# Two engines share each copy of the first transform's results, one parity each

## The chip, the cores and the metric

The kernel runs as one program on one core of a Trainium2 chip. The metric is the device time of that core in microseconds (us), the median of several runs. A core has five engines that each work through a queue of their own in order: TensorE (PE in the profile; its weight loads are listed as PEld), VectorE (DVE), ScalarE (ACT), GpSimd (POOL) and SyncE (SP), which here only starts transfers. They meet through semaphores. Matrix products land in PSUM; everything else on the core lies in SBUF; transfers between SBUF and the device's memory run on 16 DMA engines.

## The reference

The input x has 8 batches of 3136 positions by 256 channels. The attention part is the real part of a two-dimensional Fourier transform of each batch. Behind it each batch sends the 128 positions with the highest gate score through a small feed-forward network:

```
X = np.fft.fft(x, axis=1)
X = np.fft.fft(X, axis=2)
x = X.real
scores = np.einsum('bsd,d->bs', x, w_gate)
for b in range(B):
    top_idx = np.argpartition(-scores[b], capacity)[:capacity]   # capacity = 128
    xe = x[b, top_idx]
    ye = np.maximum(xe @ w1, 0.0) @ w2
    out[b, top_idx] = xe + sigmoid(scores[b, top_idx])[:, None] * ye
```

## The kernel before

The sequence of 3136 positions is split as 64 by 49, so the transform has three matrix products per batch.

**First transform** (`stage1`, lines 354 to 387). A batch of x arrives as four transfers of 1 MB (`load_to`, line 206). Mirrored rows are added in place (`fold_to`, line 345: VectorE for batch 0, GpSimd for the others). There are eight chunks per batch; each is multiplied with `w1d` into one PSUM bank `p1_{batch}_{chunk}` of 4 times 100 columns (line 372; the last chunk has 5 times 100). The 100 columns are two parities h by two halves t by 25 frequencies k. Line 373 copies a bank into the tile `uv`, in which each k has a row of 64, so neighbouring elements of the copy land 256 bytes apart. The last chunk has a second, small copy (line 375, 100 elements). The tile `zz` (line 381) holds a small side product of the same batch.

**Second and third transform** (`stage23`, line 390). Line 405 multiplies `uv` with `cuv`, six or four products to a bank. ScalarE rounds the bank to `s2h` (line 410), VectorE subtracts to get the rest `s2l` (line 411), and three products (lines 244 to 246) give the result, which VectorE or ScalarE copies to the output tile `o` (line 423). GpSimd adds a correction and the score (lines 428 to 434), SyncE stores.

**Search for the best 128** (`topk`, line 468, one per pair of batches, called A, B, C, D here). It narrows a threshold in six rounds. In the first three groups a round goes round the engines: ScalarE counts with a pass of 800 elements (`junk`, line 531, and `cth`, 532), PE sums over the partitions (`pc`, line 541), VectorE decides (`ji`, line 543) and sets the next threshold (`thr`, line 547). The next round's ScalarE pass waits for that threshold.

**Feed-forward network** (`ffn`, line 639), for pairs of batches.

A string written out by hand (`ORDER`, line 37) says in which order the pieces of these streams are written down, and so in which order each engine meets them. Nothing is reordered later: an instruction that waits holds up all that stand behind it on its engine. Seven PSUM banks are taken in turn (line 189). The first matrix product of the second transform of a batch needs the whole tile `uv`, with the copies of all eight chunks and line 375.

Of the kernel before, what the change touches and what calls it, by code (L numbers as in the profile page):

```python
# [177 lines left out]
def kernel(ctx: ExitStack, tc: tile.TileContext, x, w1, w2, wgr, tb, outs, groups, pairs):  # L178
    nc = tc.nc
# [12 lines left out]
    def bank(name, pool=psb):  # L192
        return pool.tile([128, 512], F32, tag="bank", name=name)
# [5 lines left out]
    def load_to(q):  # L199
        while len(tiles) <= min(q, 4 * NB - 1):  # L200
            b, i = divmod(len(tiles), 4)
            t = xp.tile([128, 2, 8 * 128], F32, tag="x", name=f"x_{b}_{i}")
            tiles[b, i] = t
            src = x[b, i].rearrange("p (c w) -> p c w", c=2)
            for c0, c1 in ((0, 1), (1, 2)) if b == 0 else ((0, 2),):
                nc.sync.dma_start(t[:, c0:c1], src[:, c0:c1])
# [128 lines left out]
    def fold_to(q):  # L335
        while len(folded) <= min(q, 8 * NB - 1):
            b, i = divmod(len(folded), 8)
            if i == 0:
                zs[b] = sp.tile([98, 33], F32, tag="z", name=f"z_{b}", bufs=2)
            z = zs[b]  # L340
            a0, a1 = CHUNKS[i]
            n = a1 - a0
            t = tiles[b, i // 2][0:98, i % 2]
            eng = nc.vector if b == 0 else nc.gpsimd
            eng.tensor_tensor(t[:, 0 : n * 128], t[:, 0 : n * 128], t[:, n * 128 : 2 * n * 128], op=ALU.add)  # L345
            if i % 2:
                d = tiles[b, i // 2][0:98].rearrange("p c (s d) -> p c s d", d=128)
                nc.gpsimd.tensor_copy(z[:, a0 - 4 : a0 + 4].rearrange("p (c s) -> p c s", c=2), d[:, :, 0:4, 0])  # L348
            if i == 7:
                nc.gpsimd.tensor_copy(z[:, 0:33:32], d[:, 1, 6:8, 0])  # L350
            folded.append(t)


    def stage1(b):

        uv = uvp.tile([128, 2, 25, 64], F32, tag="uv", name=f"uv_{b}")
        uvs[b] = uv
        uvt = uv.rearrange("p h k (t n) -> p h t n k", t=2)
        for i in range(8):
            if i % 2 == 0:  # L360
                load_to(4 * b + i // 2 + AHEAD)
            fold_to(8 * b + i + FOLDS)
            t = folded[8 * b + i]
            a0, a1 = CHUNKS[i]
            n = a1 - a0
            ps = bank(f"p1_{b}_{i}")[:, 0:500].rearrange("p (n c) -> p n c", n=5)
            src = ps.rearrange("p n (h t k) -> p h t n k", h=2, t=2)

            for q in range(5 if i == 7 else n):
                o = (q + 3 if i == 7 and q > 2 else q) * 128  # L370
                for r in (0, 64):
                    nc.tensor.matmul(ps[r : r + 64, q], t[:, o + r : o + r + 64], w1d, start=True, stop=True)  # L372
            nc.scalar.copy(uvt[:, :, :, a0:a1], src[:, :, :, 0:n])  # L373
            if i == 7:
                nc.scalar.copy(uvt[:, :, :, 0], src[:, :, 0, 3:5])  # L375
            yield True

        pz = bank(f"pz_{b}")[:, 0:500].rearrange("p (n c) -> p n c", n=5)
        nc.tensor.matmul(pz[0:33, 0, 0:50], zs[b], w1d[:, 50:100], start=True, stop=True)
        zz = sp.tile([33, 50], F32, tag="zz", name=f"zz_{b}", bufs=2)  # L380
        nc.scalar.copy(zz, pz[0:33, 0, 0:50])
        yield True
        nc.tensor.matmul(pz[:, 1, 0:25], zcs[:, 0:128], zz[:, 25:50], start=True, stop=False)
        nc.tensor.matmul(pz[:, 1, 0:25], zcs[:, 128:256], zz[:, 0:25], start=False, stop=True)
        nc.scalar.copy(dlt[b % 2][0], pz[:, 1, 0:25])
        nc.scalar.activation(dlt[b % 2][1], pz[:, 1, 0:25], AF.Copy, scale=wodd)
        yield True
# [305 lines left out]


    streams = {"s": (c for b in range(NB) for c in stage1(b)), "m": (c for b in range(NB) for c in stage23(b)), "w": late_setup()}
    for g, bs in enumerate(groups):
        streams["ABCD"[g]] = topk(g)
# [57 lines left out]
```

## Time and profile before

| what | value |
|---|---|
| median of 3 runs | 249.34 us (249.08 to 251.72) |
| the profiled execution's own time | 248.94 us |
| its span, first to last instruction | 247.2 us |
| PE, DVE, ACT, POOL busy share of the span | 90%, 55%, 56%, 65% |
| mean granted TensorE clock, share of full | 0.939 |
| memory traffic | 67.40 MB |

The busy shares are means over the whole span. The eight first transforms run up to about 165 us; what follows is the rest of the last batch, the search D and the feed-forward networks. Matrix products are pipelined and their ends are modelled, so a PE that reads as busy need not be at its peak.

### The profile page before, as it was taken

The page shows a single profiled execution, that of the slowest core. Times are in us where ns is not written, and L with a number is a line of the kernel's source. Part 1 is how long each engine was busy: PE and PEld are TensorE (multiplying, and loading weights), DVE is VectorE, ACT ScalarE, POOL GpSimd, SP SyncE. Part 2 cuts the span into 40 slices and gives each one's busy share as a digit, 9 for nine tenths or more (in the row PEclk, how much of TensorE's full clock was granted, in tenths as well). Part 3 has the DMA queues.
Part 4 walks back from the last instruction along what each step waited for, and adds up shares of the span by engine and source line. Part 5 has one row for each costly group of instructions (what it writes and reads, how often), then busy time and mean ns, then how long its engine had stood idle before and what let it go on. Part 6 is the DMA issues. An engine that isn't in the chain of part 4 may idle for free.

```text
span 247.2 us, 6813 instructions
## 1 busy us (share of the span) xinstructions
PE 221.3 (90%) x2672; PEld 199.8 (81%) x2672; DVE 134.8 (55%) x422; ACT 137.4 (56%) x309; POOL 160.2 (65%) x233
## 2 busy tenths in 40 slices
PE   8769999999999989997998995989999899998950
PEld 5559899989989879897987783979889798997940
DVE  1533332443553444657585558374689998943410
ACT  2544767757755887882677865877851140312300
POOL 0026799898797767965867999447958436446141
PEclk9976999999999999997999999558999999999995
DMA  6999959999999999999999899543068402011000
GB/s 226 386 407 399 400 217 361 384 414 404 406 417 319 424 405 417 414 400 399 416 420 402 301 335 382 241 160 127 0 265 248 165 22 54 26 32 43 24 22 23
DMA packets 14908, 67.40 MB, mean 273 GB/s; under 512 B 3131, under 2 KB 4892, under 8 KB 11292
## 3 DMA queue, kind: packets, MB, share of 16 engines
q1 hardware_dynamic: 13740, 64.80, 67.0%
q0 software_dynamic: 1024, 2.13, 3.4%
q8 instruction: 21, 0.34, 0.6%
q10 hardware_dynamic: 112, 0.04, 0.1%
q14 instruction: 11, 0.09, 0.1%
HBM read 39.17 MB, written 27.79 MB: 271 GB/s over the span
## 4 chain that ended last, share of the span: by engine, by line
PE 40%; DMA 25%; DVE 16%; POOL 5%; ACT 5%; issue 5%; POOLq 1%; SPq 1%; ACTq 0%
DMA spill<-sc 11%; PE p L405 10%; PE p L372 10%; DMA scr<-spill 5%; DMA xe<-out,chosen 4%; PE p L244 4%; DMA once<-in_once 3%; DMA x<-in_x 3%; PE p L246 3%; DVE junk L534 3%; PE p L245 3%; DVE o L423 2%; DVE hl L674 2%; DVE s2l L411 2%; ACT uv L373 2%
## 5 line engine op out<-in xcount | busy, mean ns | idle before, releaser
L345 POOL TENSOR_TENSOR x<-x 98x512 f32<-98x512 f32 (+1 forms) x56 | 68.9, 1245 | 8.8 <-DMA x<-in_x 7.9
L372 PE MATMUL p<-w1d,x 98*64 98x100 f32 x1056 | 58.6, 266 | 4.6 <-DVE x L345 3.4
L411 DVE TENSOR_TENSOR s2l<-p,s2h 128x390 fp32r<-128x390 f32 (+1 forms) x72 | 36.2, 530 | 46.9 <-ACT s2h L410 46.3
L373 ACT COPY uv<-p 128x400 f32<-128x400 f32 x64 | 50.5, 859 | 18.8 <-PE p L372 18.8
L372 PEld LDWEIGHTS p<-w1d,x 98*64 98x64 f32 x1056 | 52.0, 147 | 8.6 <-DVE x L345 3.7
L405 PE MATMUL p<-cuv,uv 128*64 128x130 f32 x800 | 54.7, 288 | 2.3 <-ACT uv L375 1.3
L405 PEld LDWEIGHTS p<-cuv,uv 128*64 128x64 f32 x800 | 47.3, 144 | 5.2 <-ACT uv L375 1.8
L428 POOL TENSOR_TENSOR o<-o,dl 128x384 f32<-128x384 f32 (+1 forms) x32 | 27.6, 862 | 19.3 <-DVE o L423 12.7
L410 ACT CAST s2h<-p 128x390 fp32r<-128x390 f32 (+1 forms) x72 | 31.7, 469 | 11.8 <-PE p L405 11.4
L688 POOL DMA_INDIRECT out<-xe,chosen x16 | 15.7, 980 | 22.4 <-DMA out<-xe,chosen 16.6
L423 DVE COPY o<-p 128x390 f32<-128x390 f32 (+1 forms) x48 | 23.6, 512 | 12.1 <-PE p L246 9.0
L244 PE MATMUL p<-s2h,m3h 128*128 128x390 f32 (+1 forms) x72 | 27.5, 382 | 0.2 <-ACT s2h L410 0.2
L246 PE MATMUL p<-s2l,m3h 128*128 128x390 f32 (+1 forms) x72 | 24.4, 339 | 0.0
L245 PE MATMUL p<-s2h,m3l 128*128 128x390 f32 (+1 forms) x72 | 24.1, 335 | 0.0
L531 ACT ACTIVATE junk<-scr,thr 128x800 bf16<-128x800 f32 x18 | 17.3, 962 | 10.0 <-DVE thr L547 8.9
L673 ACT ACTIVATE hh<-ph 128x256 fp32r<-128x256 f32 x32 | 12.2, 383 | 17.3 <-PE ph L246 16.6
L650 POOL DMA_INDIRECT xe<-out,chosen x16 | 15.8, 986 | 9.4 <-DVE hl L674 4.8
L244 PE MATMUL ph<-xh,w1h 128*128 128x256 f32 x64 | 19.0, 297 | 0.0
L246 PE MATMUL ph<-xl,w1h 128*128 128x256 f32 x64 | 18.3, 285 | 0.0
L245 PE MATMUL ph<-xh,w1l 128*128 128x256 f32 x64 | 18.1, 282 | 0.0
L348 POOL COPY z<-x 98x8 f32<-98x8 f32 x32 | 6.2, 195 | 16.5 <-DVE x L345 14.7
L244 PEld LDWEIGHTS p<-s2h,m3h 128*128 128x128 f32 x72 | 13.9, 193 | 3.4 <-ACT s2h L410 0.8
(132 smaller groups left out, 371.2 us busy)
## 6 DMA issues: line engine op xcount, KB each, us to landing
x<-in_x SPq DMA_DIRECT2D x28, 1024.0 KB, 12.6
out<-o SPq DMA_DIRECT2D x16, 845.0 KB, 14.1
out<-o SPq DMA_DIRECT2D x16, 780.0 KB, 9.1
x<-in_x SPq DMA_DIRECT2D x8, 512.0 KB, 6.9
scr<-spill SPq DMA_DIRECT2D x8, 200.0 KB, 9.1
w1s<-in_w SPq DMA_DIRECT2D x1, 1024.0 KB, 14.6
w2s<-in_w SPq DMA_DIRECT2D x1, 1024.0 KB, 12.1
xe<-out,chosen POOLq DMA_INDIRECT x16, 3.0
```

The costliest lines, as they stand in the source:

```text
L244: nc.tensor.matmul(out, ah, bh, start=start, stop=False)
L245: nc.tensor.matmul(out, al, bh, start=False, stop=False)
L246: nc.tensor.matmul(out, ah, bl, start=False, stop=stop)
L345: eng.tensor_tensor(t[:, 0 : n * 128], t[:, 0 : n * 128], t[:, n * 128 : 2 * n * 128], op=ALU.add)
L372: nc.tensor.matmul(ps[r : r + 64, q], t[:, o + r : o + r + 64], w1d, start=True, stop=True)
L373: nc.scalar.copy(uvt[:, :, :, a0:a1], src[:, :, :, 0:n])
L405: nc.tensor.matmul(ps[64 * h : 64 * h + 64, k * 130 : (k + 1) * 130], uv[:, h, k0 + k], cuv[:, c : c + 130], start=True, stop=True)
L410: nc.scalar.copy(h[:, 0:w], ps)
L411: nc.vector.tensor_tensor(l[:, 0:w], ps, h[:, 0:w].bitcast(F32), op=ALU.subtract)
L423: (nc.vector.tensor_copy if j % 3 else nc.scalar.copy)(o, ps)
L428: nc.gpsimd.tensor_tensor(odd, odd, dl[:, k0:k1].unsqueeze(2).to_broadcast([128, k1 - k0, 64]), op=ALU.add)
L531: nc.scalar.activation(junk, scr, AF.Sign, bias=thr, scale=-1.0, accum_out=ct)
```

## The change

One line becomes two. In place of one ScalarE copy of both parities there are two copies of one parity each: the first on ScalarE, the second on VectorE. All 64 copies of line 373 are changed; the small copy of the last chunk (375, in the changed kernel 376) stays as it is. Lines behind the change have numbers higher by one.

```
-            nc.scalar.copy(uvt[:, :, :, a0:a1], src[:, :, :, 0:n])
+            for h, copy in enumerate((nc.scalar.copy, nc.vector.tensor_copy)):
+                copy(uvt[:, h, :, a0:a1], src[:, h, :, 0:n])
             if i == 7:
                 nc.scalar.copy(uvt[:, :, :, 0], src[:, :, 0, 3:5])
```

ScalarE's order stays what it was. VectorE has 64 rows more. Three places show where they stand and what they wait for (a name such as `uv_7` is the tile of batch 7, `p1_7_5` the bank of its chunk 5; a name in brackets is the engine whose semaphore the row waits for).

VectorE before, first batch, between the last additions of x and the first `s2l`:

```order
L345 TENSOR_TENSOR x_0_3_129<-x_0_3_129 98x384 [waits DMAHW2_49]
L275 SCALAR_TENSOR_TENSOR wj0_241,cuv_132<-wg_234,cuv_132 128x129 [waits DMAHW3_49,Pool_49]
L275 SCALAR_TENSOR_TENSOR wj1_243,cuv_132<-wg_234,cuv_132 128x129 [waits DVE_49,Pool_49]
L278 TENSOR_REDUCE wodd_140<-wg_234 128x1
L279 TENSOR_TENSOR m3l_139<-once_134,m3h_138 128x128 [waits DMAHW4_49,Activation_49]
L411 TENSOR_TENSOR s2l_0_0_299<-p2_0_0_291,s2h_0_0_298 128x390 [waits Activation_49]
```

and the same place now:

```order
L345 TENSOR_TENSOR x_0_3_129<-x_0_3_129 98x384 [waits DMAHW2_49]
L374 COPY uv_0_157<-p1_0_4_228 128x2x4x25 [waits Activation_49]
L275 SCALAR_TENSOR_TENSOR wj0_246,cuv_132<-wg_239,cuv_132 128x129 [waits DMAHW3_49,Pool_49]
L275 SCALAR_TENSOR_TENSOR wj1_248,cuv_132<-wg_239,cuv_132 128x129 [waits DVE_49,Pool_49]
L278 TENSOR_REDUCE wodd_140<-wg_239 128x1
L279 TENSOR_TENSOR m3l_139<-once_134,m3h_138 128x128 [waits DMAHW4_49,Activation_49]
L374 COPY uv_0_157<-p1_0_5_254 128x2x4x25 [waits Activation_49]
L374 COPY uv_0_157<-p1_0_6_269 128x2x4x25 [waits Activation_49]
L374 COPY uv_0_157<-p1_0_7_281 128x2x3x25 [waits Activation_49]
L412 TENSOR_TENSOR s2l_0_0_307<-p2_0_0_299,s2h_0_0_306 128x390 [waits Activation_49]
```

VectorE's copy waits for ScalarE's copy of the same bank, and the last three copies of the batch stand behind the preparation of `wj`, `wodd` and `m3l`.

ScalarE now, at the same place, the last chunk of the first batch:

```order
L374 COPY uv_0_157<-p1_0_5_254 128x2x4x25 [waits PE_49]
L374 COPY uv_0_157<-p1_0_6_269 128x2x4x25 [waits PE_49]
L374 COPY uv_0_157<-p1_0_7_281 128x2x3x25 [waits PE_49]
L376 COPY uv_0_157<-p1_0_7_281 128x2x2x25 [waits DVE_49]
L382 COPY zz_0_297<-pz_0_295 33x50 [waits PE_49]
```

The small copy (376), which waited for nothing but the copy ahead of it on its own engine, now waits for VectorE, in every batch, and `zz` stands behind it.

VectorE before, in the last batch, where the search C runs beside the last chunks:

```order
L543 SCALAR_TENSOR_TENSOR ji_2_2322,inc_2_2321<-pc0_2_2383,ts_2_2316 128x16 [waits PE_49]
L547 TENSOR_SCALAR thr_2_2318<-inc_2_2321,lo_2_2311,ts_2_2316 128x1 [waits DVE_49,Activation_49]
L537 TENSOR_SCALAR lo_2_2311<-lo_2_2311,inc_2_2321 128x1 [waits DVE_49]
L564 TENSOR_TENSOR md_1_2406<-sc1_148,pb_1_2391 128x50 [waits PE_49]
L565 TENSOR_TENSOR md_1_2406<-sc1_148,pb_1_2391 128x50
L566 TENSOR_TENSOR md_1_2406<-md_1_2406 128x50 [waits DVE_49]
L569 SCALAR_TENSOR_TENSOR ss_1_2410<-begin_950,md_1_2406 128x100 [waits DVE_49]
L543 SCALAR_TENSOR_TENSOR ji_2_2322,inc_2_2321<-pc1_2_2422,ts_2_2316 128x16 [waits PE_49]
```

and now:

```order
L538 TENSOR_SCALAR lo_2_2369<-lo_2_2369,inc_2_2379 128x1 [waits DVE_49]
L374 COPY uv_7_2259<-p1_7_4_2456 128x2x4x25 [waits Activation_49]
L565 TENSOR_TENSOR md_1_2467<-sc1_148,pb_1_2451 128x50
L566 TENSOR_TENSOR md_1_2467<-sc1_148,pb_1_2451 128x50
L567 TENSOR_TENSOR md_1_2467<-md_1_2467 128x50 [waits DVE_49]
L570 SCALAR_TENSOR_TENSOR ss_1_2471<-begin_979,md_1_2467 128x100 [waits DVE_49]
L374 COPY uv_7_2259<-p1_7_5_2473 128x2x4x25 [waits Activation_49]
L544 SCALAR_TENSOR_TENSOR ji_2_2380,inc_2_2379<-pc1_2_2484,ts_2_2374 128x16 [waits PE_49]
```

The copy of chunk 4 stands ahead of the four rows of `md` and `ss`, and the copy of chunk 5 between them and `ji`, VectorE's decision in the second round of the search C.

## Rows read from the trace of the kernel before

**Rows 1.** The page, busy us (share of the span) and instructions of each engine.

```profile
PE 221.3 (90%) x2672; PEld 199.8 (81%) x2672; DVE 134.8 (55%) x422; ACT 137.4 (56%) x309; POOL 160.2 (65%) x233
```

**Rows 2.** Two stretches: busy us of PE, PEld, DVE, ACT, POOL; clock; DMA share; GB/s.

```profile
100.00:110.00 10.00, 9.88 (x150) 8.86 (x148) 5.26 (x19) 8.61 (x18) 7.95 (x13) 1.00 1.02 413
...
160.00:170.00 10.00, 9.22 (x98) 8.37 (x94) 5.84 (x19) 7.50 (x18) 6.13 (x9) 0.55 0.45 176
```

**Rows 3.** Who waited for whom, PE: us in total, times, longest.

```profile
PE p L405 <- ACT uv L375: 1.3, 2, 0.8
```

**Rows 4.** Groups by line and shape: busy us, mean ns | idle ahead.

```profile
L373 ACT COPY uv<-p 128x400 f32<-128x400 f32 x56 | 45.2, 883 | 16.3 <-PE p L372 16.3
L410 ACT CAST s2h<-p 128x390 fp32r<-128x390 f32 x56 | 26.3, 495 | 9.4 <-PE p L405 9.0
...
L375 ACT COPY uv<-p 128x100 f32<-128x100 f32 x8 | 3.1, 387 | 0.0
...
L423 DVE COPY o<-p 128x390 f32<-128x390 f32 x32 | 17.2, 556 | 7.3 <-PE p L246 6.3 <-PE pc L541 1.1
...
L423 DVE COPY o<-p 128x260 f32<-128x260 f32 x16 | 6.4, 423 | 4.8 <-PE p L246 2.7 <-PE pc L541 2.0
```

**Rows 5.** Timeline at 18 us: start, length, instruction, idle ahead and its releaser.

```profile
18.06 0.28 DVE L279 TENSOR_TENSOR m3l<-once,m3h 128x128 fp32r<-128x128 f32 x1
18.48 0.36 ACT L375 COPY uv<-p 128x100 f32<-128x100 f32 x1
...
18.89 4.50 PE L405 MATMUL p<-cuv,uv 128*64 128x130 f32 x48 [1.02 <-ACT zz L381]
```

**Rows 6.** Timeline at 88 us, batch 4's last chunk.

```profile
87.76 1.03 DVE L411 TENSOR_TENSOR s2l<-p,s2h 128x390 fp32r<-128x390 f32 x2 [3.06 <-ACT s2h L410]
...
87.99 0.69 ACT L373 COPY uv<-p 128x300 f32<-128x300 f32 x1
...
88.63 0.26 ACT L381 COPY zz<-pz 33x50 f32<-33x50 f32 x1
...
88.94 0.40 PE L383 MATMUL pz<-zz,zcs 33*128 33x25 f32 x2 [0.64 <-ACT zz L381]
```

**Rows 7.** Timeline at 101 us, search A beside batch 5's chunk 3.

```profile
101.08 0.17 DVE L543 SCALAR_TENSOR_TENSOR ji<-pc,ts 128x16 f32<-128x16 f32 x1
...
101.38 0.87 ACT L373 COPY uv<-p 128x400 f32<-128x400 f32 x1 [0.90 <-PE p L372]
...
102.05 0.95 ACT L531 ACTIVATE junk<-scr,thr 128x800 bf16<-128x800 f32 x1
...
103.47 0.17 PE L541 MATMUL pc<-cth,same 128*128 128x16 f16 x1
```

**Rows 8.** Timeline at 136 us, batch 6's last chunk.

```profile
136.16 0.66 ACT L373 COPY uv<-p 128x300 f32<-128x300 f32 x1 [0.68 <-PE p L372]
...
136.62 0.37 ACT L375 COPY uv<-p 128x100 f32<-128x100 f32 x1
...
137.04 2.88 PE L405 MATMUL p<-cuv,uv 128*64 128x130 f32 x48 [0.48 <-ACT uv L375]
```

**Rows 9.** Timeline at 158 us, search C beside batch 7's last chunks.

```profile
157.96 0.20 DVE L564 TENSOR_TENSOR md<-sc,pb 128x50 bf16<-128x50 f32 x1
...
158.52 0.37 DVE L569 TENSOR_TENSOR_SCAN ss<-begin,md 128x100 bf16<-128x100 bf16 x1
...
159.18 0.81 ACT L373 COPY uv<-p 128x400 f32<-128x400 f32 x1
...
160.34 0.17 DVE L543 SCALAR_TENSOR_TENSOR ji<-pc,ts 128x16 f32<-128x16 f32 x1 [1.45 <-PE pc L541]
...
161.00 0.96 ACT L531 ACTIVATE junk<-scr,thr 128x800 bf16<-128x800 f32 x1
...
162.72 0.17 PE L541 MATMUL pc<-cth,same 128*128 128x16 f16 x1
...
165.70 4.49 PE L405 MATMUL p<-cuv,uv 128*64 128x130 f32 x48 [0.78 <-ACT uv L375]
```

## The prediction, made before the changed kernel was run

> **What bounds the kernel now.** Read first the page's busy shares [rows 1]: PE stands at 221.3 us of a 247.2 us span, VectorE at 134.8 and ScalarE at 137.4. Both evacuating engines look half idle, and nearly equally so. Then the busy times by stretch [rows 2]: around 100 us PE shows 9.88 of 10 us and the DMA engines are full (share 1.02), so up to there the array and the transfers run level, and ScalarE follows close behind with 8.61. Third, who waited for whom: PE's wait for the copies into `uv` is 1.3 us in two places [rows 3], and its waits for `zz`, which stands behind those copies on ScalarE, are 1.02 us [rows 5] and 0.64 us [rows 6]. So all that a faster copy could give back to PE directly is about 3.0 us. The copies take 45.2 us of ScalarE in their common shape [rows 4], but nearly all of that lies beside PE's work.
>
> What matters is order and delay: every engine runs its list in order, and the searches go ScalarE, PE, VectorE, ScalarE in each round. A time is gained or lost where an engine in such a ring, or the last copy of a batch, comes later than before.
>
> **The price of a copy.** On ScalarE the copies of 100 and 400 elements take 387 and 883 ns [rows 4], a line of 1.65 ns per element above some 222 ns. That gives 552 ns for 200 elements and 470 for the 150 of a last chunk. ScalarE gets back 0.33 us in each of 56 copies and a little less in 8: about 20 us in all. On VectorE no copy with this scattered output exists. Its nearest rows are its copies out of PSUM of 390 and 260 elements, 556 and 423 ns [rows 4]: 1.02 ns per element above 157 ns, so 361 ns for 200 and 310 for 150. That is the low end, since those rows write neighbouring elements. The high end is ScalarE's slope for the scattered output, 157 + 200 times 1.65 = 487 ns. I take 0.36 and 0.31 us, the same engine's rows, and keep 0.49 for the range. VectorE thus grows by 56 times 0.36 plus 8 times 0.31, some 23 us, to about 157 us; ScalarE falls to about 117. Neither becomes the bound by its sum.
>
> A scattered write has a rule of its own. ScalarE's rows show it: 883 ns for 400 scattered elements against 495 for 390 neighbouring ones [rows 4]. The Trainium skill ("SBUF — State Buffer", Door 1: The DMA port swizzle) says that SBUF has lines of 16 bytes and that each access to a new line pays a penalty; as it speaks of the memory, it would hold for VectorE too. By VectorE's rows the sum below stands; by that rule the high end would be the right one, which is worked out among the rivals.
>
> **The halves do not run side by side.** VectorE's copy waits for ScalarE's copy of the same bank, as the order shows. One bank is emptied after 0.55 + 0.04 + 0.36 = 0.95 us in place of 0.88, the 0.04 being about what lies between ScalarE's last copy (136.62 + 0.37) and PE's start at 137.04 [rows 8]. For runs of three chunks the two engines overlap and the last is done sooner, but PE hardly waits for banks. So I cost ScalarE's 20 us of relief at nothing: the array's own work hides it. Were that cover gone, it would be worth at most the 3.0 us above.
>
> **Where VectorE's copies come onto the path.** Five places, in order of time, each against the trace with everything ahead equally late.
>
> 1. *First batch.* The copies of chunks 5, 6 and 7 stand behind `m3l`, which ends at 18.06 + 0.28 = 18.34 [rows 5]. Then 0.36 + 0.36 + 0.31 gives 19.37; the small copy waits for that: + 0.05 + 0.36; PE starts + 0.05 later, at 19.83, where it started at 18.89. **+0.9 us**. The stores and loads that SyncE issues wait for what PE makes from here on, so I let this stand.
> 2. *Batch 4's last chunk.* VectorE is in two `s2l` from 87.76 to 88.79 [rows 6] when its copy of the last chunk comes due: 89.10. Small copy 89.5, `zz` behind it (its end was 0.03 us behind the small copy's), so PE's product with `zz` starts at about 89.6 where it was 88.94. **+0.65 us**.
> 3. *Search A beside batch 5.* `ji`, at 101.08 [rows 7], now stands behind VectorE's copy of chunk 3, whose ScalarE half runs from 101.38 to 101.93. So VectorE's ends at 102.33 and `ji` comes 1.2 us late. From `ji` to the next ScalarE pass the trace shows 0.66 us (160.34 to 161.00) [rows 9]: 102.98 where it was 102.05, ScalarE having then been held by its longer copy. Of these 0.9 us I take 0.8, as neighbours overlap a little; PE's `pc` at 103.47 came straight behind that pass. **+0.8 us**.
> 4. *Batch 6's last chunk.* From ScalarE's start to PE's start were 0.88 us [rows 8], with the two ScalarE copies overlapped by 0.2. Now 0.47 + 0.31 + 0.37 and three hops of 0.05 give 1.30. **+0.4 us**.
> 5. *Search C beside batch 7.* The copy of chunk 4 (ScalarE half from 159.18 to 159.73 [rows 9]) ends on VectorE at 160.13. Behind it now stand the four rows from 157.96 to 158.89, which were done long before: 161.06. Then the copy of chunk 5: 161.42. Only then `ji`, which was at 160.34: 1.08 us late, and the next pass on ScalarE with it, at 162.08 in place of 161.00. `pc` follows a pass by 1.42 us (102.05 to 103.47) [rows 7], so 163.50 in place of 162.72, + 0.78. From `pc` to the second transform were 2.98 us [rows 9], now longer by the 0.4 of place 4: PE starts at 166.9 in place of 165.70. **+1.15 us**.
>
> Behind that no chunk is left; the last batch, search D and the networks follow as before, later by the sum: 0.9 + 0.65 + 0.8 + 0.4 + 1.15 = 3.9 us. The profiled execution's own time is 248.94 us, 0.4 below the median of the three runs, so **252.8 us**, 1.4% above the median. I call 1%, some 2.5 us, what a measurement can tell from no change.
>
> **Rivals.**
>
> *The middle delays are taken back.* With the transfers full [rows 2], a PE that is 0.8 us late may only find its data sooner, and the next wait is shorter. Then what counts is what falls where the transfers thin out (share 0.45 at 160 us [rows 2]): places 4 and 5, 1.55 us, so 250.5. For it: the share of 1.02. Against it: around 100 us PE is as full as they are, and no row shows it waiting for a transfer.
>
> *The scattered output costs VectorE what it costs ScalarE.* Then each copy on those paths is longer by 0.13 us (0.10 for a last chunk): three at the first place, two at the second, two or three at the third, one at the fourth, three at the fifth, about 1.4 us: 254.2. The rule on SBUF lines named above speaks for this one; no row of before has VectorE writing so.
>
> *Faster: ScalarE was what held the array.* With 0.33 us less in each copy, ScalarE reaches the small copy, `zz` and the passes of the searches sooner. If VectorE's halves are picked up at once, because VectorE has idled ahead of most of them, the 3.0 us of PE's waits named at the start go: 245.9. More could come from the clock: from 160 to 170 us it is granted at 0.55 [rows 2], near the lower of its two levels (1.2 of 2.4 GHz), behind PE's waits in search C, and the same work at full clock would take some 4.5 us less. It decides at `ji` of search C: if that comes sooner than before relative to its `pc`, this case holds; if later, not. Against it stands the order, which puts two copies and four other rows ahead of it.
>
> **Chances and range.** My forecast 0.48, the longer VectorE copy 0.08, the delays taken back 0.32, faster 0.12. So slower by over 1% 0.56, within 1% 0.32, faster by over 1% 0.12. The forecast's own range is 251.8 (two of the places failing) to 254.2. The whole range runs from 249.0 (all but nothing left of the five) to 255.2 (the longer copy, and another search round of a microsecond that I did not see); below it lies the faster case, above it little.
>
> **What would show it.** ScalarE's copies at about 0.55 us, VectorE's new rows at 0.36 (0.49 by the rival), each starting some 0.04 us behind the end of ScalarE's. ScalarE's busy time near 117 us, VectorE's near 157. The first product of the second transform at 19.8 us in place of 18.89. The last batch's second transform starting near 169.6 us (165.70 + 3.9). In search C a `ji` a microsecond behind its `pc`, with a copy ending just ahead of it. Behind that start the stretch to the end should be as long as before, 81.5 us. The prediction is wrong if the last batch's second transform starts within 1 us of where it was, if PE's clock comes back in the stretch of 160 to 170 us, or if VectorE's copies turn out to run beside ScalarE's.

## The result and the profile after

The changed kernel takes 250.86 us (median of 19 runs, 249.09 to 253.29); the kernel before took 249.73 in 19 runs beside it (246.18 to 252.03). The ratio is 1.0122, with a 95% interval of 1.0083 to 1.0161: slower, by less than 2%. This ratio, like those of the experiments, takes of each kernel only the runs within 1.5% of its own fastest, and as the kernel before has five of 19 runs under 247.5 us and the changed one none, it is larger than the difference of the medians (1.1 us). The means of all 19 runs differ by 1.6 us, give or take 1.0 (95%). The profiled executions took 250.57 and 248.94 us: 1.6 us more.

The page of the changed kernel, busy us of each engine (answers to [rows 1]):

```profile
PE 222.3 (89%) x2672; PEld 200.3 (80%) x2672; DVE 158.3 (64%) x486; ACT 122.6 (49%) x309; POOL 160.4 (64%) x233
```

The groups of the copies, by shape (answers to [rows 4]):

```profile
L374 ACT COPY uv<-p 128x200 f32<-128x200 f32 x56 | 28.0, 526 | 18.2 <-PE p L372 17.6
L374 DVE COPY uv<-p 128x200 f32<-128x200 f32 x56 | 27.2, 516 | 19.5 <-ACT uv L374 19.1
L374 ACT COPY uv<-p 128x150 f32<-128x150 f32 x8 | 3.4, 430 | 4.9 <-PE p L372 4.9
L374 DVE COPY uv<-p 128x150 f32<-128x150 f32 x8 | 3.3, 415 | 3.9 <-ACT uv L374 3.9
L376 ACT COPY uv<-p 128x100 f32<-128x100 f32 x8 | 2.7, 332 | 4.9 <-DVE uv L374 3.2 <-DVE ji L544 1.7
```

VectorE's busy time went to 158.3 us (157 forecast), ScalarE's to 122.6 (117 forecast). ScalarE's half costs 526 ns (552 forecast). VectorE's row lasts 516 where 361 was forecast. And the wait is there: 19.1 us of VectorE's idle time is spent waiting for ScalarE's half of the same bank, and the small copy waits for VectorE 4.9 us in all. Who waited for whom, PE (answers to [rows 3]):

```profile
PE p L406 <- ACT uv L376: 2.0, 2, 1.1
PE p L406 <- ACT zz L382: 1.7, 1, 1.7
PE pc L542 <- ACT cth L533: 1.6, 3, 1.0
PE p L246 <- DVE s2l L412: 0.9, 1, 0.9
```

The five places in the timeline of the changed kernel. The first batch (answers to [rows 5]):

```profile
18.33 0.28 DVE L279 TENSOR_TENSOR m3l<-once,m3h 128x128 fp32r<-128x128 f32 x1
18.53 1.08 DVE L374 COPY uv<-p 128x200 f32<-128x200 f32 x3
19.64 0.33 ACT L376 COPY uv<-p 128x100 f32<-128x100 f32 x1 [1.04 <-DVE uv L374]
...
20.02 1.35 PE L406 MATMUL p<-cuv,uv 128*64 128x130 f32 x10 [1.72 <-ACT zz L382]
```

From the end of `m3l` (18.61) to PE's start are 1.41 us; they were 0.55 (18.34 to 18.89 in [rows 5]). The three copies of VectorE last 0.49, 0.49 and 0.41 us, but start 0.33 us apart, so together they take 1.08.

Batch 4's last chunk, search A, batch 6's last chunk and search C (answer to [rows 6 to 9]):

```profile
90.78 0.40 PE L384 MATMUL pz<-zz,zcs 33*128 33x25 f32 x2 [0.59 <-ACT zz L382]
...
103.56 0.51 DVE L374 COPY uv<-p 128x200 f32<-128x200 f32 x1 [0.83 <-ACT uv L374]
103.92 0.17 DVE L544 SCALAR_TENSOR_TENSOR ji<-pc,ts 128x16 f32<-128x16 f32 x1
...
105.96 0.17 PE L542 MATMUL pc<-cth,same 128*128 128x16 f16 x1 [0.97 <-ACT cth L533]
...
137.45 0.33 ACT L376 COPY uv<-p 128x100 f32<-128x100 f32 x1 [0.48 <-DVE ji L544]
...
137.83 1.44 PE L406 MATMUL p<-cuv,uv 128*64 128x130 f32 x22 [0.87 <-ACT uv L376]
...
160.13 0.49 DVE L374 COPY uv<-p 128x200 f32<-128x200 f32 x1 [1.65 <-ACT uv L374]
...
161.31 0.47 DVE L374 COPY uv<-p 128x200 f32<-128x200 f32 x1
161.63 0.16 DVE L544 SCALAR_TENSOR_TENSOR ji<-pc,ts 128x16 f32<-128x16 f32 x1
...
162.21 0.96 ACT L532 ACTIVATE junk<-scr,thr 128x800 bf16<-128x800 f32 x1 [0.97 <-DVE thr L548]
```

Each `ji` stands right behind a copy, as forecast. PE now waits 0.97 us for search A at 105.96, where it had waited 0.12.

But the lateness does not simply add up. For the same product of PE, take its start in a kernel less its start in the kernel before (median over the products that start in the 3 us from each point; points in time of the kernel before). This table carries the rest of the document; the experiments are explained below it:

| kernel | 19 us | 25 | 85 | 88 | 100 | 103 | 118 | 124 | 136 | 148 | 151 | 166 | 199 |
|---|---|---|---|---|---|---|---|---|---|---|---|---|---|
| changed | 1.13 | 1.35 | 1.59 | 1.84 | 1.63 | 2.48 | -0.73 | 0.37 | 0.79 | 0.83 | -0.17 | 1.31 | 1.44 |
| e1 batch 0 only | 0.70 | 0.79 | 0.96 | 0.94 | 0.95 | 0.95 | 0.97 | 0.96 | 0.96 | 0.96 | 0.04 | -2.91 | -2.71 |
| e2 no last chunk | -0.01 | 0.99 | 0.73 | 0.40 | 0.38 | 1.22 | -1.98 | -0.94 | -0.91 | -0.91 | -1.42 | -1.42 | -1.45 |
| e3 batches 1 to 3 | 0.25 | 0.97 | 1.14 | 1.15 | 1.15 | 1.15 | 1.24 | 1.22 | 1.22 | 1.22 | 0.29 | 0.80 | 1.28 |
| e4 VectorE first | 1.16 | 1.13 | 1.30 | 1.98 | 3.18 | 3.49 | 0.29 | 1.63 | 1.79 | 1.79 | 0.63 | -2.03 | -2.15 |
| e5 dense output | 0.57 | 1.59 | 1.71 | 1.86 | 1.66 | 2.42 | -0.78 | 0.17 | 1.32 | 2.19 | -0.25 | 0.45 | 1.52 |
| e6 whole copies | 1.22 | 1.57 | 1.42 | 1.58 | 1.40 | 2.07 | -0.32 | 0.66 | 1.15 | 1.19 | 0.24 | -1.05 | -1.45 |
| f1 before, again | 0.01 | 0.72 | 1.13 | 1.13 | 1.16 | 1.15 | 2.35 | 2.82 | 3.61 | 4.44 | 2.21 | -0.19 | 1.89 |
| f2 changed, again | 0.85 | 0.69 | 0.50 | 0.78 | 0.60 | 1.45 | -1.75 | -0.71 | -0.30 | -0.30 | -1.19 | -0.19 | 1.41 |
| g1 lh moved, no split | 0.02 | 0.21 | 0.34 | 0.36 | 0.37 | 0.40 | -2.78 | -1.34 | -0.44 | 0.18 | -1.88 | -4.61 | -4.72 |
| g2 lh moved, all split | 1.19 | 1.20 | 1.51 | 1.80 | 1.60 | 2.45 | -0.75 | 1.09 | 1.58 | 1.61 | 0.03 | 2.16 | 3.45 |
| g3 lh moved, 35 split | 0.17 | 0.15 | 0.39 | 0.06 | 0.03 | 0.02 | -3.11 | -1.66 | -0.76 | -0.12 | -2.15 | -4.92 | -5.37 |
| g4 last chunks only | 0.50 | 1.22 | 1.36 | 1.98 | 1.77 | 1.79 | 3.08 | 3.44 | 4.72 | 5.23 | 2.90 | 0.72 | 2.28 |

In the row of the changed kernel the steps of the five places are seen: 1.13 at 19 us (1.35 by 25), 0.25 at 88, 0.85 at 103, 0.4 at 136, and 0.8 between 160 and 166 us (0.51 to 1.31). Between 25 and 80 us nothing is added.

Up to 192 us f1 and f2 are the kernel before and the changed kernel once more, so their rows show what a second execution gives. Steps that come from a wait repeat: 0.28 at 88 us, 0.85 at 103, -3.20 by 118 and 0.4 at 136 in f2. Stretches of low clock do not: f1, which splits nothing, is 1.13 us late at 85 us and 4.44 at 148 (its clock is low from 115.9 to 122.7 and from 139.8 to 143.2 us). So a number of this table is read as a step with its wait, not as a sum. The 1.13 at 19 us also holds 0.27 by which `m3l` itself ends later; its end lies between 18.15 and 18.85 us in the fourteen traces, split or not.

And there are steps that the prediction did not have: **-3.2 us between 103 and 118, +1.1 at 124, -1.0 at 151**, and +0.7 from 151 to 160, where the clock fell at 153.5 us in place of 155.4.

The first of these is read from two engines. Search A ends with two tiny VectorE rows, `lh`. In the kernel before they stand beside GpSimd's additions (VectorE, GpSimd and PE rows of its timeline):

```profile
111.29 1.21 DVE L553 TENSOR_SCALAR lh<-se,lo 128x2 f32<-128x2 f32 x1
112.41 0.88 DVE L554 TENSOR_SCALAR lh<-se,hi 128x2 f32<-128x2 f32 x1
...
111.19 1.28 POOL L345 TENSOR_TENSOR x<-x 98x512 f32<-98x512 f32 x1
112.43 0.83 POOL L428 TENSOR_TENSOR o<-o,dl 128x384 f32<-128x384 f32 x1
...
113.34 0.39 PE L557 MATMUL pb<-lh,onesf 128*128 128x4 f32 x2 [1.35 <-DVE lh L554]
...
115.00 3.63 PE L372 MATMUL p<-w1d,x 98*64 98x100 f32 x48
```

Each `lh` ends within 0.04 us of the GpSimd row beside it (112.50 and 112.47, 113.29 and 113.26). In the changed kernel the same rows come when GpSimd's additions are just ending, at 113.83, and a later row, `pi`, is caught instead (same engines):

```profile
113.71 0.22 DVE L554 TENSOR_SCALAR lh<-se,lo 128x2 f32<-128x2 f32 x1
113.84 0.22 DVE L555 TENSOR_SCALAR lh<-se,hi 128x2 f32<-128x2 f32 x1
...
111.31 2.52 POOL L345 TENSOR_TENSOR x<-x 98x512 f32<-98x512 f32 x2
...
114.31 0.28 PE L558 MATMUL pb<-lh,onesf 128*128 128x4 f32 x2
...
121.58 1.18 DVE L586 SCALAR_TENSOR_TENSOR pi<-pa 128x50 int32<-128x50 f32 x1
...
120.15 2.54 POOL L345 TENSOR_TENSOR x<-x 98x512 f32<-98x512 f32 x2
```

`pi` took 0.21 us before and 1.18 now; it ends at 122.76, GpSimd's additions at 122.69. That is the wait of 0.9 us for `s2l` above, and the +1.1 at 124.

The clock goes with it. The stretches 110 to 120 and 160 to 170 us, before (the second was in [rows 2]):

```profile
110.00:120.00 10.00, 8.65 (x103) 7.80 (x102) 6.12 (x22) 4.18 (x9) 6.77 (x10) 0.83 1.02 397
```

and now:

```profile
110.00:120.00 10.00, 10.00 (x145) 9.04 (x143) 7.69 (x30) 5.96 (x16) 8.53 (x13) 1.00 1.02 406
160.00:170.00 10.00, 8.56 (x84) 7.50 (x82) 6.54 (x25) 5.94 (x18) 3.53 (x6) 0.50 0.56 219
```

Behind the wait for `lh` PE ran at the lower level from 114.4 to 117.8 us (48 products in 3.63 us, 2.28 now); without that wait the clock stays up. This holds in all fourteen traces: both `lh` are caught in the five kernels that have them on VectorE and no split copy ahead of search A's `ji` (before, e1, e3, f1, g4), and in each the clock falls behind them, between 114.4 and 116.4 us; in the other nine it does not fall there. Of the 3.2 us about 1.6 are the two rows (1.21 + 0.88 less 0.44), the rest the clock behind them.

### The profile page after: what moved, and what is told of

The parts are those of the page before. It is cut to its first block, busy times and chain, and to the rows that moved or that the text cites. A ratio compares the mean times of both kernels' runs of the same rounds, so it can differ in the third digit from the quotient of the medians.

```text
span 248.8 us, 6882 instructions
## 1 busy us (share of the span) xinstructions
PE 222.3 (89%) x2672; PEld 200.3 (80%) x2672; DVE 158.3 (64%) x486; ACT 122.6 (49%) x309; POOL 160.4 (64%) x233
## 4 chain that ended last, share of the span: by engine, by line
PE 37%; DVE 23%; DMA 21%; ACT 6%; issue 5%; POOL 5%; POOLq 1%; SPq 0%; ACTq 0%; DVEq 0%
PE p L406 12%; PE p L372 8%; DMA x<-in_x 6%; DMA scr<-spill 5%; DMA out<-o 5%; DMA spill<-sc 3%; PE p L244 3%; DVE uv L374 3%; DVE s2l L412 2%; PE p L246 2%; PE p L245 2%; DVE junk L535 2%; DVE o L424 2%; ACT junk L532 2%; DMA xe<-out,chosen 2%
## 5 line engine op out<-in xcount | busy, mean ns | idle before, releaser
L412 DVE TENSOR_TENSOR s2l<-p,s2h 128x390 fp32r<-128x390 f32 (+1 forms) x72 | 36.3, 530 | 24.3 <-ACT s2h L411 22.3
L374 DVE COPY uv<-p 128x200 f32<-128x200 f32 x64 | 30.3, 503 | 23.4 <-ACT uv L374 23.0
L374 ACT COPY uv<-p 128x200 f32<-128x200 f32 x64 | 31.5, 514 | 23.1 <-PE p L372 22.6
L244 PE MATMUL ph<-xh,w1h 128*128 128x256 f32 x64 | 19.1, 298 | 0.0
```

Source lines behind the costliest of these rows:

```text
L244: nc.tensor.matmul(out, ah, bh, start=start, stop=False)
L374: copy(uvt[:, h, :, a0:a1], src[:, h, :, 0:n])
L412: nc.vector.tensor_tensor(l[:, 0:w], ps, h[:, 0:w].bitcast(F32), op=ALU.subtract)
```

## The experiments

Three theories were held against each other: the cost lies in a few **places** on the path (P), it is the **load** of the copies, spread evenly (L), or it is **taken back** or made by the clock (T, A, C). Twelve kernels ran in three groups of four; the kernel before had a median of 249.72 us beside the first group (e1 to e4), 248.90 beside the second (f1, f2, e5, e6) and 253.39 beside the third (g1 to g4).

**e1, batch 0 alone**

```
+            if b == 0:
+                for h, copy in enumerate((nc.scalar.copy, nc.vector.tensor_copy)):
+                    copy(uvt[:, h, :, a0:a1], src[:, h, :, 0:n])
+            else:
+                nc.scalar.copy(uvt[:, :, :, a0:a1], src[:, :, :, 0:n])
```

> The copies are split in batch 0 alone (8 of 64). Theory P (places: the time comes from VectorE's halves that stand behind other VectorE work or ahead of it on the path): the second transform of batch 0 starts at about 20.0 us as in the changed kernel (18.89 before), and what follows keeps that 1.1 us: ratio to before 1.004 to 1.005. Theory L (load: every split copy costs the same 3.0/64 = 0.047 us, wherever it stands): 8 copies, +0.4 us, ratio 1.0015, and no single start moves by over 0.4. Theory T (taken back: the array waits for x behind it anyway): the start is at 20.0, but the next anchors (the search A's passes at 84 us) stand where they stood, ratio 1.000.

Median 249.14 us, ratio 1.0055 (1.0005 to 1.0105). The start is at 19.59, 0.70 late (1.41 us behind `m3l`, as in the changed kernel), and the table keeps 0.95 from 85 us up to 148, then loses 0.92 where PE waits for the gathered rows of the feed-forward network. P for the step; L falls; T is right only at 151 us. What follows there is the clock: it is low from 163.1 to 166.5 us in this profile, and was from 155.4 to 169.0 in the kernel before, which is the -2.9.

```profile
160.00:170.00 10.00, 8.36 (x100) 7.69 (x101) 6.62 (x17) 8.28 (x25) 7.63 (x11) 0.83 0.46 179
```

**e2, all but the last chunks** (as e1, with another condition)

```
-            if b == 0:
+            if i != 7:
```

> The copies are split in the chunks 0 to 6 of every batch, the last chunk is whole on ScalarE again (56 of 64 split). Theory P: the chain ScalarE, VectorE, ScalarE ahead of the second transform is gone; batch 0 still waits for two halves behind m3l (start near 19.6 instead of 20.0), the product with zz in batch 4 loses its step of 0.6, batch 6's start its 0.4, batch 7's start 0.4; the searches A and C keep theirs. Of the 3.0 us about 1.6 are left: ratio 1.006. Theory L: 56/64 of 3.0 = 2.6 us, ratio 1.0105.

Median 248.83 us, ratio 1.013 (1.0093 to 1.0168); the two point opposite ways, and the total decides nothing. The steps do: no step at 19 us, none at 136, 0.84 at 103 as in the changed kernel. P had expected a start of batch 0 near 19.6; that was wrong (18.74), and so is the sentence that the first product of the second transform needs the whole tile `uv`. The first product reads parity 0 alone, which is ScalarE's, and starts while VectorE is still copying parity 1:

```profile
18.16 0.82 DVE L375 COPY uv<-p 128x200 f32<-128x200 f32 x2
...
18.74 1.64 PE L409 MATMUL p<-cuv,uv 128*64 128x130 f32 x11 [0.78 <-ACT zz L385]
```

What makes it wait in the changed kernel is the small copy (376) on ScalarE, which waits for VectorE's last half, with `zz` behind it. At 88 us the lateness falls by 0.33, because PE no longer waits for `zz`; ahead of that it waits for a bank that VectorE still copies:

```profile
88.01 0.44 PE L244 MATMUL p<-s2h,m3h 128*128 128x390 f32 x1 [0.16 <-DVE uv L375]
...
89.34 0.40 PE L387 MATMUL pz<-zz,zcs 33*128 33x25 f32 x2
```

(0.64 us of idle before it in [rows 6]). Here ScalarE's relief is worth something.

**e3, batches 1 to 3**

```
-            if b == 0:
+            if b in (1, 2, 3):
```

> The copies are split in batches 1, 2 and 3 alone (24 of 64): no search runs beside most of them and nothing of the preparation stands on VectorE. Theory P: no place of the five lies here; only the chains of the last chunks, which PE does not wait for there: ratio 1.000 (within 0.002). Theory L: 24 times 0.047 = 1.1 us, ratio 1.0045.

Median 250.48 us, ratio 1.0169 (1.0087 to 1.0251), above both theories; six runs can't tell such sizes here. Its trace can: 0.97 us late at 25, before any split copy stands on a path (the low clock of the first batch ends at 24.0 us, before at 22.3), and 1.15 at 103. 24 split copies add nothing from 25 to 80 us. L falls again.

**e4, VectorE first**

```
-            for h, copy in enumerate((nc.scalar.copy, nc.vector.tensor_copy)):
+            for h, copy in enumerate((nc.vector.tensor_copy, nc.scalar.copy)):
```

> All 64 copies split, but VectorE takes its half first and ScalarE's waits for it. Busy times of both engines stay as in the changed kernel (158 and 123 us). Theory L: the same load, the same time as the changed kernel, ratio 1.012. Theory P: ScalarE, whose queue holds the passes of the searches, zz and s2h, now stands still until VectorE is through: in batch 0 m3l ends at 18.6, three halves of VectorE (0.45, 0.45, 0.40), ScalarE's last half 0.45 and the small copy 0.37 give a start at 20.7 instead of 20.0; every other place is at least as late as in the changed kernel. Ratio 1.018 to 1.03.

Median 250.37 us, ratio 1.0181 (1.0115 to 1.0247). The interval takes in P's 1.018 and L's 1.012, and the medians differ by 0.65 us: the total decides nothing. Two sentences of P were wrong: the first batch starts at 20.05, not 20.7, and the step of search A at 103 is 0.31, less than the changed kernel's 0.85. In its place batch 4's step is 0.68, and the clock was low from 91.6 to 95.0 us, behind a wait of 1.16 us for `zz` at 90.76. The order inside the pair only moves the cost.

**f1 and f2, PE's wait filled**

```
             pt = bank(f"pxt_{nm}_{i}")
+            for _ in range((12, 8)[i] if bs[0] == 2 else 0):
+                nc.tensor.matmul(pt[:, 256:512], wz[:, 0:128], wz, start=True, stop=True)
```

> The kernel before, with 12 and 8 products of zeros (128x256) ahead of the two pairs of transposes in front of the second feed-forward network, where PE waits for the gathered rows (1.66 and 1.29 us idle before 152.39 and 153.99 in the kernel before). Theory C (the clock): the times of the kernel before fall into two groups, 245 to 247 and 249 to 253 us, because PE's clock falls behind this wait in most runs and stays at 0.50 up to about 168 us, and in the others not; in the first four profiles of this study with the fall at 153 to 155 the stretch 160 to 170 stands at 0.50 to 0.62, in the two without it at 0.83. With the wait filled the clock stays at 1.00 from 150 to 160, and the runs gather at 245 to 247.5: median about 246.3, 3.4 us under the median of before. Theory N: the fall has another cause, or the products can't start ahead of the transposes; then both groups stay, and the median stays near 249.7, or is 1 us more by the products themselves.

> The changed kernel with the same filling. None of 19 runs of the changed kernel lay under 249. Theory C: its runs gather too, and the difference to the filled kernel before is what the change costs at an equal clock. Theory P (the places cost what the profile pair shows: +1.1 in batch 0, +1.3 at the last second transform, some 3 us taken back at 113 us, where two rows of lh on VectorE wait for GpSimd before and not after): f2 minus f1 is 1.0 to 2.0 us, about 247.8. Theory A (all is clock): f2 minus f1 is within 0.4 us. Theory L (load, 3.0 us spread over all copies): f2 minus f1 is 3.0 us.

Both missed what they aimed at. The wait at 151 to 154 us belongs to the first network (batches 0 and 1), and the edit put the products ahead of the second, where PE did not wait: they ran from 192.4 to 197.3 us, 20 of them:

```profile
L658 PE MATMUL pxt<-wz 128*128 128x256 bf16 x20 | 2.5, 274 | 0.0
```

So theory C and N stay untested, and what makes the clock fall late in one run and not in another stays open. The medians are 250.78 and 251.70 us, ratios 1.0039 (0.9982 to 1.0096) and 1.0185 (1.0124 to 1.0246): with the same extra 1.2 us at 192 us in both, the change costs 0.9 us by the medians, near P's lower end, and 1.5% by the ratios, near L: undecided. What the two do give is a second pair of traces, the rows of the table.

**e5, VectorE's output dense** (values of VectorE's half land at wrong places)

```
-            for h, copy in enumerate((nc.scalar.copy, nc.vector.tensor_copy)):
-                copy(uvt[:, h, :, a0:a1], src[:, h, :, 0:n])
+            nc.scalar.copy(uvt[:, 0, :, a0:a1], src[:, 0, :, 0:n])
+            half = uv.rearrange("p h k x -> p (h k x)")[:, 1600 + 200 * i : 1800 + 200 * i]
+            nc.vector.tensor_copy(half.rearrange("p (t n k) -> p t n k", t=2, n=4), src[:, 1, :, 0:4])
```

> The changed kernel, but VectorE writes its half to neighbouring elements of uv (200 at a time, in the last chunk too), so values land at wrong places; counts, waits and order stay. Theory D (the scattered output is what made VectorE's copy cost 516 ns for 200 elements): the rows fall to about 0.36 us, VectorE's busy time from 158 to about 149; the second transform of batch 0, behind three such copies, starts 0.3 us earlier (19.7 in place of 20.0), batch 6's and 7's 0.1 earlier; the total is 0.3 to 1.0 under the changed kernel: ratio to before 1.008 to 1.011. Theory S (the shape of the access to PSUM, or the wait itself, sets the price): the rows stay above 0.48 us, and the total at 1.012.

The row of the copy:

```profile
L375 DVE COPY uv<-p 128x200 f32<-128x200 f32 x64 | 22.5, 362 | 24.3 <-ACT uv L373 24.2
```

362 ns: the scattered output alone makes the difference to 516. The start of batch 0 is at 19.46 (20.02 in the changed kernel), but 0.39 of that is an earlier `m3l`; behind `m3l` it comes after 1.24 us in place of 1.41. Search A's step is 0.76 in place of 0.85. Median 250.06 us, ratio 1.0101 (1.0034 to 1.0167). Theory D holds in the rows; the total lies where D put it, but its interval takes in the 1.0122 of the changed kernel too.

**e6, whole copies in turn**

```
+            copy = nc.vector.tensor_copy if i % 2 else nc.scalar.copy
+            copy(uvt[:, :, :, a0:a1], src[:, :, :, 0:n])
```

> No copy is split; the even chunks are whole on ScalarE, the odd ones whole on VectorE (32 copies of 400 or 300 elements). No copy waits for another of the same bank, but for the small one. Theory P (order on VectorE's queue): the copies of chunks 5 and 7 of batch 0 stand behind m3l: 18.5 + 0.88 + 0.69 + 0.36 gives a start at 20.5 (18.89 before, 20.0 in the changed kernel); in the searches a whole copy of 0.88 us stands ahead of ji, +0.9 at A and C: ratio 1.012 to 1.020. Theory S (the serial pair, VectorE behind ScalarE in each bank, is the cost): it is gone, ratio 1.004 or less. Theory L (the load on VectorE): VectorE's busy time is about 163, as in the changed kernel or above: ratio 1.012.

Median 249.87 us, ratio 1.0105 (1.0049 to 1.0162). With no copy waiting for another but the small one, the start of batch 0 is at 20.11 (P had 20.5) and search A's step 0.67 (P had 0.9): the same two places, nearly the same sizes. So S falls: the pair in series is not the cost, VectorE's queue is. Its copies of 400 scattered elements took 867 ns, ScalarE's 870:

```profile
L374 DVE COPY uv<-p 128x400 f32<-128x400 f32 x24 | 20.8, 867 | 6.4 <-PE p L372 6.3
```

**g1, g2, g3: `lh` on ScalarE**

```
-            nc.vector.tensor_scalar(lh[:, 0:n], c_one, lo, None, op0=ALU.mult)
-            nc.vector.tensor_scalar(lh[:, n : 2 * n], c_one, hi, None, op0=ALU.mult)
+            nc.scalar.activation(lh[:, 0:n], c_one, AF.Copy, scale=lo)
+            nc.scalar.activation(lh[:, n : 2 * n], c_one, AF.Copy, scale=hi)
```

g1 has no split copy, g2 all 64, g3 those under `if b not in (0, 5, 7) and i != 7`.

> The kernel before with the two small lh rows of each search on ScalarE in place of VectorE. Behind search A they took 1.21 and 0.88 us on VectorE, each ending with a GpSimd row beside it (0.22 and 0.22 in the changed kernel), PE waited 1.35 us for them, and its clock fell from 114.4 to 117.8 us behind that wait. Theory G (these two rows and the clock behind them are the 3.2 us that the changed kernel wins back between 109 and 119 us): lh takes about 0.3 us each on ScalarE, pb starts 1.2 us earlier than 113.34 relative to the search ahead of it, and if the clock doesn't fall the second transform behind it is 2.5 to 3.2 us earlier. At the end 1 to 3 us are left: median 247 to 248.5. Theory N (the wait only moves: PE then waits for x or for s2l): less than 0.5 us are left at 130 us.

> The changed kernel with lh on ScalarE. Theory P with G: lh was quick there already, so its time is that of the changed kernel within 0.7 us (250.2 to 251.5), and against the kernel before with lh on ScalarE it shows the places alone, with nothing won back at 113 us: 1.3 (batch 0) + 0.3 + 0.8 + 0.4 + 0.8 = 3.6 us, less what the wait for the gathered rows at 151 us absorbs (up to 1.0): 2.6 to 3.6 us. Theory L (load): the difference between the two is the same 2.0 us as between the kernels without this edit.

> As g1, with the copies split in the chunks 0 to 6 of batches 1, 2, 3, 4 and 6 alone: 35 of 64 copies, none of them at one of the five places. Theory P: such copies cost nothing; start by start within 0.3 us of g1 up to 150 us, time within 0.7 us of it. Theory L: 35 times 0.047 = 1.6 us more than g1, spread over these batches. If ScalarE's relief is worth anything where VectorE's half is in nobody's way, this kernel is below g1.

In g1 (ScalarE, then PE):

```profile
111.55 0.30 ACT L553 ACTIVATE lh<-se,lo 128x2 f32<-128x2 f32 x1 [1.19 <-DVE lo L548]
111.80 0.30 ACT L554 ACTIVATE lh<-se,hi 128x2 f32<-128x2 f32 x1
...
112.21 0.33 PE L557 MATMUL pb<-lh,onesf 128*128 128x4 f32 x2
113.58 2.28 PE L372 MATMUL p<-w1d,x 98*64 98x100 f32 x48
```

The kernel that splits nothing wins the very step of the changed kernel: 0.40 to -2.78 between 103 and 118, 3.2 us, PE's wait and the low clock both gone. So the -3.2 does not come from faster copies, but from where `lh` falls beside GpSimd, which search A's lateness of 0.85 us changes; theory G holds. It does not last in g1: `pi` is caught too (1.17 us, from 119.89), +1.4 at 124, and the clock is low from 135.3 to 138.7 us, some +1.5, so that 0.18 is left at 148; the end is open to the clock. The median is 252.84 us beside 253.39, ratio 0.9925 (0.9841 to 1.0009): 0.5 us by the medians, under the 1 to 3 expected. (This whole group ran longer than the others: between 205 and 217 us its four profiles lose 2.5 to 4 us against the kernel before, split or not. In search D PE waits 1.5 to 1.9 us for `lh` and 0.6 to 2.2 for `pc`, where it waited 0.3 and 0.2, and its clock is then low for 3.4 to 6.8 us from 207 (g1, g3) or 215 us (g2, g4); what made these waits longer stays open.)

g3 follows g1 within 0.4 us at every point up to 166 us, from 88 us on ahead of it, with 35 copies split. P holds, L (1.6 us) falls: copies away from the places cost nothing, and in batch 4 they win the 0.33 us at `zz`. Median 250.80 us, ratio 0.9942 (0.9883 to 1.0002), the lowest median of its group; by the ratios it is the same as g1.

g2 shows the places with nothing new won back at 113: against g1, 1.2 at 19 us, 0.3 at 88, 0.8 at 103. Its median is 255.90 us, ratio 1.0148 (1.0071 to 1.0225): 3.1 us above g1 by the medians, in the 2.6 to 3.6 of P. The time of the changed kernel, 250.2 to 251.5, was missed with the whole group. With twelve and six runs that scatter by 7 and 4 us, this size is supported rather than shown; the two profiles themselves lie 9.6 us apart, most of it from 151 to 170 us, where the clock is low in g2 (from 160.0 on) and not in g1.

**g4, the last chunks alone**

```
-            if b == 0:
+            if i == 7:
```

> The copies are split in the last chunk of each batch alone (8 of 64). Theory P: the three steps of the last chunk's chain and no other: the product with zz in batch 4 +0.3 to +0.6, batch 6's second transform +0.4, batch 7's +0.4; in batch 0 the half waits for m3l, +0.3; no step at 103 us in search A (0.84 in the changed kernel). Together 1.2 to 1.6 us. Theory L: 8 times 0.047 = 0.4 us and no step.

Median 254.35 us, ratio 1.013 (1.0063 to 1.0196). Steps: 0.5 at 19, 0.62 at 88, none at 103, PE's wait in batch 6 up from 0.48 to 0.97, in batch 7 from 0.78 to 1.15. Batch 4's place is the one forecast, the copy behind two `s2l` (VectorE, then PE):

```profile
89.12 1.03 DVE L415 TENSOR_TENSOR s2l<-p,s2h 128x390 fp32r<-128x390 f32 x2 [3.06 <-ACT s2h L414]
90.07 0.40 DVE L375 COPY uv<-p 128x150 f32<-128x150 f32 x1
...
90.92 0.40 PE L387 MATMUL pz<-zz,zcs 33*128 33x25 f32 x2 [1.27 <-ACT zz L385]
```

P in the steps and about in the total (1.0 us by the medians, 1.2 to 1.6 expected); L (0.4 and no step) falls by the steps. The steps of g4, g1 and g3 at 118 to 148 us also hold stretches of low clock (116.4 to 123.2 and 140.3 to 143.7 in g4).

## Why the prediction held, and where it did not

- **What bounds it, and the direction.** Right: slower, by places where VectorE's queue delays a ring or the last copy of a batch, with next to nothing for the relief of ScalarE in between. e3 and g3 show the last part: outside the places 35 copies cost nothing and won 0.33 us. How much of the delay is left at the end changes with the clock from execution to execution: the profiled run took 1.6 us more than before in the first pair, and 0.4 us less in f2 than in f1.
- **The time.** Missed: 252.8 us forecast, 250.86 measured, below the forecast's own range of 251.8 to 254.2; the whole range, 249.0 to 255.2, is wide enough to hold it. That the ratio of 1.0122 comes near the forecast's 1.4% is in part luck: the medians differ by 0.45%.
- **The price on VectorE.** A term that was mis-sized: 516 ns, not 361. The rival of the longer copy, which I gave 0.08, was right about the price, and e5 shows why. The Trainium skill ("SBUF — State Buffer", Door 1: The DMA port swizzle) had the rule, a penalty for each new line of 16 bytes; the trace agrees (516 scattered, 362 dense). It was worth little in time, 0.1 us in search A and 0.17 in the first batch, because copies in a row overlap: three took 1.08 us, where the forecast had 1.03 and the rival 1.39.
- **Place 1** (+0.9): +0.86 from the end of `m3l` to PE's start (1.41 us in place of 0.55; e1, f2 and g2 1.40 to 1.42, e2, f1 and g1 0.50 to 0.55). **Place 3** (+0.8): 0.85, in e2 0.84 and in f2 and g2 0.85; nothing in the kernels without a split copy there. **Place 4** (+0.4): 0.39, and none in e2. **Place 5** (+1.15): about 0.8 in this pair; 1.6 to 1.7 in f2, e5 and g2, whose clock falls at another time. These four came as described, with the rows in the order that was forecast.
- **Place 2** (+0.65): 0.25, and not by the forecast's path alone. Ahead of the product with `zz` PE is 0.30 later, where it waits 0.15 us for a bank that VectorE still copies; the prediction said that PE hardly waits for banks. At `zz` it then waits 0.59 us in place of 0.64. Alone, as in g4, the last chunk costs the 0.62 that was forecast; with the earlier chunks split as well and the last one whole (e2, g3) the 0.64 are gone. So "ScalarE's 20 us of relief at nothing" was wrong at this one place: 0.30 + 0.59 - 0.64 = 0.25. By 94 us 0.2 of it is made good.
- **The sum.** 1.35 + 0.25 + 0.85 + 0.4 + 0.8 make 3.65 us (with 0.86 for the first, 3.16), near the forecast 3.9. What failed is the sentence that the last batch follows "later by the sum": its second transform came at 167.0, 1.3 us late. Between lie +0.25 at 82 us, which e1, e3 and f1 show in like size with no split copy near, -0.2 at 94, -3.2 at 113, +1.1 at 124, -1.0 at 151, where PE's wait for gathered rows absorbs what came before, and +0.7 by the earlier fall of the clock: 1.3. The prediction's sign of being wrong was less than 1 us there; this pair passes it narrowly, and by luck: in the second pair the same product starts at 165.51 us in both f1 and f2, whose stretches of low clock differ. From 167.0 to the end the stretch was as long as before, 81.8 us (81.5).
- **The rival "taken back"** (250.5 us, 0.32) comes nearest to the median of 250.86, but its mechanism, a PE that finds x sooner, was not what happened. What did is in the rows: `lh` and `pi` end with GpSimd's row. The Trainium skill ("SBUF — State Buffer", SBUF: two separate sides) has a rule that fits: VectorE and GpSimd share a pair of ports, which the one that starts first holds for its whole instruction while the other waits; on VectorE's side it speaks of rows in a two-port mode or with two inputs in SBUF. In the three pairs shown above the trace agrees, within 0.1 us; whether `lh` runs in such a mode no run here tests. The prediction left GpSimd's 65% out of account.
- **The clock in 160 to 170 us.** That it does not come back held in this pair (0.55 to 0.50), but in e1 it stood at 0.83 with the late start of batch 0 unchanged. A good part of the scatter of all these kernels, 245 to 258 us, goes with the clock (time and mean granted clock of the runs of the kernel before correlate at -0.87 to -0.92 in the three groups), and why it falls for longer in one run than in another was not found.

## What to carry to other kernels

Cost a moved copy by its place in the other engine's queue, not by its duration: 35 copies away from the rings cost nothing, the other 29 some 3 us of delay where they stand. A short row on VectorE beside long rows on GpSimd can cost several times its length, and a shift ahead of it decides whether it does; look for such rows before judging an edit by its total. Where totals scatter by 3%, compare starts of the same product between traces, step by step, name the wait behind each step, and profile the same kernel twice to see which steps repeat.

## What was not expected of the hardware

- VectorE's copy from PSUM to elements 256 bytes apart takes as long as ScalarE's: 516 and 526 ns for 200, 867 and 870 for 400 elements; dense 362 ns for 200.
- Copies in a row on VectorE start 0.33 us apart though each lasts 0.49.
- Rows of 2 or 50 elements on VectorE took 0.2 us alone and up to 1.3 us beside GpSimd; in the fourteen traces each `lh` or `pi` row over 0.3 us ended within 0.1 us of the end of a GpSimd row.
- A wait of PE of 1.35 us was followed by 3.4 us at the lower clock level, so that it cost about twice its length.
